# Sixteen filler matmuls as steps of TensorE's own order, and all step orders chosen anew, in a recurrent attention followed by a mixture of experts

## The chip, the cores and the metric

One core of one Trainium2 chip. The metric is the device time of one execution in microseconds; the median of several runs counts. PE is TensorE, ACT ScalarE, DVE VectorE, POOL GpSimd, SP SyncE. A "step" below is an entry of the kernel's plan: a handful of instructions that are issued together.

## The reference, cut to what matters

```
f = 1 / (1 + exp(-f_logit))                       # all of q, k, v, f: (4, 8, 768, 48)
for t in range(768):
    state = f[:, :, t, :, None] * state + einsum('bhd,bhe->bhde', k[:, :, t], v[:, :, t])
    y[:, :, t] = einsum('bhd,bhde->bhe', q[:, :, t], state)
x = y.transpose(0, 2, 1, 3).reshape(3072, 384)
p = domain_probs / (domain_probs.sum(-1, keepdims=True) + 1e-09)
for e in range(4):                                # w1[e]: 384 x 1024, w2[e]: 1024 x 384
    out += p[:, e:e+1] * (maximum(x @ w1[e], 0) @ w2[e])
```

## The kernel before, in words

The sequence is cut into six chunks (c = 0 to 5) of 128 tokens; a step's name ends in chunk and batch, so `q 0.2` is chunk 0, batch 2. Attention of a chunk is done in matrix form. For chunk 0 and each batch the steps are, in the order in which one needs the other:

- `ld f`, `ld k`, `ld q` (loads on SP's queue, 192 KB each) and `v issue` (POOL's queue, with a cast to bf16);
- `gate1`, `gate2` on ACT (exp and ln of the gate), then `cs` and `cq` on PE (cumulative sums over time, L388 to L399), then `exps` and `expq` on ACT;
- the products `k` and `q` (L434, L431), on DVE or POOL;
- `tpk`, `tpq` on PE (transposes, L443), `ev_tp` (their copy out of PSUM, on ACT or DVE), `at` on PE (scores, L474);
- `ev_at0`, `ev_at1`: scores out of PSUM with the causal mask, on DVE (L486); for the two named in `BYPOOL` ACT copies (L482) and POOL masks (`mask1`, L478);
- `y` on PE (L501), `ev_y`, `xt` on PE (transpose, L526), `ev_xt`: the chunk's part of x for the experts;
- `kv` on PE (L507), `ev_kv` on DVE (L514), four `sf` steps on POOL (L519, L522): the state for the next chunk.

The expert part has `h` (x times w1; in chunk 0's first expert twelve matmuls in a group, later three, L535; from chunk 1's second half `hs`, L567), `relu`, and either `o` (h times w2, L550) or seven products `p` (L626, L635) of a Strassen-like scheme with sums `s` of h and sums `t` of w2 on DVE. Attention of the next chunk runs among the experts of the last one. Weights come in twelve pieces `w 0` to `w 11` on POOL's queue: `w 0` and `w 1` serve `h 0.0`, `w 2` and `w 3` `h 0.1`, `w 4` and `w 5` the products `p 0.d0`, `w 6` `h 0.2`, `w 7` `p 0.d1`, `w 8` `h 0.3`. `pp` and `probs` prepare the expert probabilities, from `ld p`.

The order of the work is written out: `STEPS` holds for each of PE, ACT, DVE, POOL and DMA a list of step numbers. An engine runs its list strictly in that order, and which list a step is in says which engine does it. `Plan.run` walks the lists to give out buffers and the order of emission; `GATE` and `SEQ` name which of the loads a `v` issue waits for and in what sequence v and w are issued.

Fillers are matmuls of 128 x 128 by 512 on a constant tile (`busy`) into a PSUM bank that is kept free for them (`SPARE`) until the first `h`. They have no use but to keep PE at work. Before, they hang on other steps, as a count that is issued just ahead of the step:

```
FILL = ((("cs", "cq"), 6), (("tpq", "tpk"), 4))
for kinds, n in FILL:
    next(o for o in done if o.engine == "PE" and o.name.split()[0] in kinds).pad = n
for o in done:
    for _ in range(o.pad):
        nc.tensor.matmul(out=spare, lhsT=busy[:, 0:128], rhs=busy, start=True, stop=True)
    o.ins = o.emit(o.engine)
```

So six stand ahead of the first `cs` and four ahead of the first transposes (L1083).

Of the kernel before, what the change touches and what calls it, by code (L numbers as in the profile page):

```python
# [34 lines left out]
    ),  # L35
    "ACT": (
# [10 lines left out]
    ),  # L47
    "DVE": (
# [15 lines left out]
    ),  # L64
    "POOL": (
# [6 lines left out]
    ),  # L72
    "DMA": (
# [109 lines left out]
def kernel(  # L183
# [11 lines left out]
    nc = tc.nc  # L195
# [29 lines left out]
    P = Plan(rooms)  # L225
# [845 lines left out]
    for kinds, n in FILL:  # L1071
        next(o for o in done if o.engine == "PE" and o.name.split()[0] in kinds).pad = n
# [59 lines left out]
```

## Time and profile before

| | |
|---|---|
| median of three runs | 288.67 us (286.22, 288.67, 290.31) |
| profiled execution | 287.4 us; its span 285.7 us |
| mean granted PE clock | 0.994 |
| busy: PE, weight loads, DVE | 277.8 us (97%), 242.4 us (85%), 220.2 us (77%) |
| busy: ACT, POOL | 159.8 us (56%), 111.3 us (39%) |
| chain that ended last | PE 92%, SP's queue 3%, DMA 2% |
| HBM read, written | 31.51 MB, 4.72 MB |

The span runs from the first to the last instruction of the profiled execution; its own time is 1.7 us longer. Busy time of PE is counted from issue to a modelled end, so matmuls that follow each other overlap in it. "The head" below is what comes before the stretch in which PE has no idle time any more, that is, the first 24 us.

### The profile page before, as it was taken

What the parts mean: (1) busy time and instruction counts of PE and PEld (TensorE: products, weight loads), DVE (VectorE), ACT (ScalarE), POOL (GpSimd) and SP (SyncE); (2) the same over time, 40 slices, a digit from 0 to 9 for tenths busy, and PEclk for the clock granted to TensorE, in tenths of its full rate; (3) what the DMA queues carried; (4) which work ended last, traced back from release to release, by engine and by line L of the source; (5) the groups of instructions that cost most, each with busy time, mean ns of one, the idle gap of its engine ahead of it and who ended that gap; (6) DMA issues with size and microseconds to landing.
All of it is one profiled execution on the core that took longest, in us unless ns stands there. A gap on an engine that the chain in (4) does not pass through costs nothing.

```text
span 285.7 us, 7671 instructions
## 1 busy us (share of the span) xinstructions
PE 277.8 (97%) x3100; PEld 242.4 (85%) x3100; DVE 220.2 (77%) x463; ACT 159.8 (56%) x320; POOL 111.3 (39%) x189
## 2 busy tenths in 40 slices
PE   6989999999999999999999999999999999999994
PEld 3678676668987999999999999998998999999994
DVE  5769898987889799885888867866976888554873
ACT  5763366687874868463955838754723632534410
POOL 5759000658269540738607344375436000000000
PEclk9979999999999999999999999999999999999999
DMA  6999999999969989999799869997562080461003
GB/s 148 208 201 207 207 208 212 185 186 202 211 117 149 196 160 194 212 187 209 145 167 202 163 130 174 213 157 131 101 105 67 1 112 2 110 140 28 2 2 111
DMA packets 153847, 41.87 MB, mean 147 GB/s; under 512 B 144316, under 2 KB 153020, under 8 KB 153812
## 3 DMA queue, kind: packets, MB, share of 16 engines
q1 hardware_dynamic: 142548, 34.66, 62.8%
q0 software_dynamic: 11264, 6.72, 16.8%
q8 instruction: 24, 0.39, 0.6%
q14 instruction: 11, 0.09, 0.1%
HBM read 31.51 MB, written 4.72 MB: 127 GB/s over the span
## 4 chain that ended last, share of the span: by engine, by line
PE 92%; SPq 3%; DMA 2%; DVE 1%; issue 1%; ACT 0%; DVEq 0%
PE ps_m L567 33%; PE ps_m L626 29%; PE ps_m L535 11%; PE ps_m L550 6%; PE ps_m L635 5%; PE ps_m L474 2%; DMA q<-in_q_dram 2%; PE ps_m L501 2%; SPq L336 1%; PE ps_m L507 1%; PE ps_m L497 1%; SPq L338 1%; PE ps_m L384 1%; PE ps_m L443 1%; PE ps_m L526 0%
## 5 line engine op out<-in xcount | busy, mean ns | idle before, releaser
L567 PE MATMUL ps_m<-x,w_sb 128*128 128x256 bf16 x864 | 105.6, 273 | 0.0
L575 ACT ACTIVATE h<-ps_m 128x512 bf16<-128x512 f32 x98 | 54.8, 599 | 67.2 <-PE ps_m L567 47.1
L567 PEld LDWEIGHTS <-w_sb 128*128 128x128 bf16 x864 | 82.3, 98 | 9.0
L626 PEld LDWEIGHTS <-S 128*128 128x128 bf16 x584 | 48.5, 98 | 1.2
L654 DVE TENSOR_TENSOR o<-ps_m,o 128x192 f32<-128x192 f32 x92 | 30.7, 351 | 18.4 <-PE ps_m L626 17.0
L573 DVE TENSOR_SCALAR h<-ps_m 128x512 bf16<-128x512 f32 x46 | 31.0, 686 | 10.8 <-PE ps_m L567 10.6
L434 POOL TENSOR_TENSOR qk<-q,e 128x384 bf16<-128x384 f32 x19 | 22.7, 1197 | 38.7 <-ACT e L417 26.4
L626 PEld LDWEIGHTS <-h 128*128 128x128 bf16 x432 | 36.6, 98 | 0.9
L535 PE MATMUL ps_m<-x,w_sb 128*128 128x128 bf16 (+2 forms) x264 | 35.6, 283 | 0.0
L457 ACT ACTIVATE yb<-ps_m,pn 128x384 bf16<-128x384 f32 x49 | 26.3, 597 | 6.3 <-PE ps_m L501 6.1
L490 DVE TENSOR_TENSOR AT<-ps_m,mask 128x512 bf16<-128x512 f32 x40 | 25.7, 684 | 4.6 <-PE ps_m L474 4.5
L626 PE MATMUL ps_m<-ts_sb,S 128*128 128x192 bf16 x288 | 29.2, 246 | 0.0
L522 POOL TENSOR_TENSOR Sf<-Sf,egs 48x192 f32<-48x192 f32 x40 | 20.5, 517 | 21.9 <-DVE S L590 12.3
L626 PE MATMUL ps_m<-w_sb,h 128*128 128x192 bf16 x288 | 28.8, 246 | 0.0
L626 PE MATMUL ps_m<-w_sb,S 128*128 128x192 bf16 (+1 forms) x296 | 28.6, 244 | 0.0
L546 ACT ACTIVATE h<-ps_m 128x512 bf16<-128x512 f32 (+1 forms) x44 | 19.8, 489 | 15.3 <-PE ps_m L535 12.5
L535 PEld LDWEIGHTS <-w_sb 128*128 128x128 bf16 x264 | 21.6, 98 | 7.6
L590 DVE TENSOR_TENSOR S<-h 128x1024 bf16<-128x1024 bf16 x36 | 24.6, 694 | 2.5 <-ACT h L575 1.6
L417 ACT ACTIVATE e<-ps_m 128x384 f32<-128x384 f32 x40 | 23.4, 705 | 4.8 <-PE ps_m L384 4.8
L434 POOL TENSOR_TENSOR qk<-k,e 128x384 bf16<-128x384 f32 x19 | 18.9, 1000 | 10.3 <-DMA k<-in_k_dram 5.0
L550 PE MATMUL ps_m<-w_sb,h 128*128 128x384 bf16 x96 | 18.1, 326 | 0.0
L349 POOL DMA_DIRECT2D w_sb<-in_moe_w_dram x12 | 9.6, 801 | 21.2 <-DMA k<-in_k_dram 21.2
(95 smaller groups left out, 372.6 us busy)
## 6 DMA issues: line engine op xcount, KB each, us to landing
out_dram<-o SPq DMA_DIRECT2D x23, 192.0 KB, 2.4
q<-in_q_dram SPq DMA_DIRECT2D x10, 384.0 KB, 5.6
k<-in_k_dram SPq DMA_DIRECT2D x10, 384.0 KB, 5.2
v<-in_v_dram SPq DMA_DIRECT2D x10, 384.0 KB, 5.1
f<-in_f_logit_dram SPq DMA_DIRECT2D x9, 384.0 KB, 5.5
w_sb<-in_moe_w_dram POOLq DMA_DIRECT2D x8, 384.0 KB, 7.6
w_sb<-in_moe_w_dram POOLq DMA_DIRECT2D x4, 768.0 KB, 14.1
f<-in_f_logit_dram SPq DMA_DIRECT2D x6, 192.0 KB, 3.9
```

The source lines that it names most:

```text
L417: nc.scalar.activation(out=o, in_=i, func=AF.Exp, scale=1.0 if j else -1.0)
L434: return engines[eng].tensor_tensor(out=tl("qk", c, b)[:, j, :, 0:D].rearrange("t (i r) d -> t i r d", r=2), in0=tl("qk"[j], c, b // 2)[:, ...
L457: nc.scalar.activation(out=ys, in_=y, func=AF.Copy, scale=pe)
L490: nc.vector.tensor_tensor(out=tl("AT", c, b)[:, r].rearrange("s i t -> s (i t)"), in0=tl("A", c, b, r).rearrange("s i t -> s (i t)"), in1= ...
L535: nc.tensor.matmul(out=hp(c, e, fc, n0, n1, nf)[:, f], lhsT=w1_sb[:, e, kk, (fc + f) * 128:(fc + f + 1) * 128], rhs=tl("xT", c)[:, kk, n0: ...
L550: nc.tensor.matmul(out=tl("op", c, e, nt)[:, 0:Din], lhsT=tl("h", c, e, half_of(c, nt * T))[:, fc, nt * T:(nt + 1) * T], rhs=w2_sb[:, e, f ...
L567: nc.tensor.matmul(out=out_[:, f], lhsT=w1_sb[:, e, kk, (fc + f) * 128:(fc + f + 1) * 128], rhs=tl("xs", c, hf, p)[:, el, kk, :], start=(k ...
L573: nc.vector.tensor_relu(out=dst, in_=tl("hp", c, hf, p, el, fc))
L575: nc.scalar.activation(out=dst, in_=tl("hp", c, hf, p, el, fc), func=AF.Relu)
L590: return nc.vector.tensor_tensor(out=o, in0=in0, in1=in1, op=op)
L626: nc.tensor.matmul(out=out_, lhsT=lhs[:, f, :], rhs=rhs[:, f, cols], start=(first and el == 0 and f == 0), stop=(el == 1 and f == KH - 1), ...
L654: nc.vector.tensor_tensor(out=o, in0=src, in1=o, op=ALU.add)
```

## The change

The ten hanging fillers (`pad`, `FILL`) go. Sixteen become steps of their own, `fl 0` to `fl 15`, one matmul each, which stand in PE's list wherever the list puts them. All five lists are other ones (steps behind the fillers have numbers higher by 16). `BYPOOL` becomes "0.1 2.1": the second half of batch 0's scores, instead of batch 1's, is copied by ACT and masked by POOL. `SEQ` and `GATE`: `v 1` is issued ahead of `v 0`; `v 1` waits for `k 0.0` and `v 0` for `k 0.2` (before, `v 0` for `k 0.1` and `v 1` for `k 0.2`).

```diff
-        self.pad, self.number = 0, None
+        self.number = None
...
+    def filler():
+        return nc.tensor.matmul(out=spare, lhsT=busy[:, 0:128], rhs=busy, start=True, stop=True)
+
+    for i in range(FILLERS):
+        P.add(f"fl {i}", {"PE": 0.22}, lambda _: filler(), -190 + i, frees=[SPARE])
...
-    for kinds, n in FILL:
-        next(o for o in done if o.engine == "PE" and o.name.split()[0] in kinds).pad = n
...
-        for _ in range(o.pad):
-            nc.tensor.matmul(out=spare, lhsT=busy[:, 0:128], rhs=busy, start=True, stop=True)
...
-FILL = ((("cs", "cq"), 6), (("tpq", "tpk"), 4))
+FILLERS = 16
-SEQ = "v0 v1 v2 w0 v3 w1"
-BYPOOL = "1.1 2.1"
+SEQ = "v1 v0 v2 w0 v3 w1"
+BYPOOL = "0.1 2.1"
-GATE = {"v0": (0, "k", 1), "v1": (0, "k", 2)}
+GATE = {"v1": (0, "k", 0), "v0": (0, "k", 2)}
```

The lists of the head, with names in place of numbers. PE, before (`6 fl` and `4 fl` are the hanging ones) and after:

```
before: 6 fl, cs 0.1, cs 0.0, cq 0.1, cq 0.0, 4 fl, tpk 0.1, tpq 0.1, tpk 0.0, tpq 0.0, at 0.1, cs 0.3, at 0.0, cq 0.3,
        cs 0.2, cq 0.2, y 0.0, tpk 0.3, pp, tpq 0.3, tpk 0.2, y 0.1, tpq 0.2, xt 0.0, at 0.3, xt 0.1, kv 0.1, at 0.2,
        kv 0.0, h 0.0.0.128, y 0.3, h 0.0.0.0, kv 0.3, xt 0.3, y 0.2, xt 0.3, kv 0.2, h 0.0.4.0, xt 0.2, h 0.0.0.384 ...
after:  fl 11, 13, 1, 6, 4, 14, cs 0.0, cq 0.0, cs 0.1, cq 0.1, tpk 0.0, tpq 0.0, fl 10, fl 9, tpk 0.1, cs 0.3, tpq 0.1,
        cq 0.3, at 0.0, fl 5, at 0.1, fl 7, fl 3, fl 12, cs 0.2, cq 0.2, pp, tpk 0.3, y 0.1, kv 0.1, fl 8, tpq 0.3, fl 15,
        y 0.0, tpk 0.2, tpq 0.2, xt 0.1, at 0.3, xt 0.0, fl 2, at 0.2, fl 0, kv 0.0, h 0.0.0.0, y 0.3, h 0.0.0.128,
        kv 0.3, xt 0.3, y 0.2, xt 0.3, kv 0.2, h 0.0.4.128, xt 0.2, h 0.0.4.384 ...
```

SP's loads (all but `p` with chunk 0):

```
before: f1 f0 q1 k0 k1 k2 q0 f3 f2 k3 p q3 q2
after:  f0 f1 k0 f3 q0 k2 k1 q1 k3 f2 q3 p q2
```

POOL:

```
before: v issue 0, 1, 2, w issue 0, v issue 3, k 0.3, w issue 1, mask1 0.1, w issue 2, 3, 4, mask1 0.2, w issue 5, 6, 7,
        sf 0.0.0, sf 0.1.0, sf 0.3.0, sf 0.3.1, w issue 8 ...
after:  k 0.0, v issue 1, 0, 2, w issue 0, v issue 3, w issue 1, 2, mask1 0.0, w issue 3, 4, 5, mask1 0.2, sf 0.0.0,
        w issue 6, sf 0.3.0, sf 0.1.0, sf 0.0.1, sf 0.1.1, w issue 7, 8 ...
```

DVE and ACT:

```
before DVE: k 0.1, k 0.0, q 0.1, q 0.0, ev_tp 0.1, ev_tp 0.0, ev_at0 0.1, ev_at1 0.0, ev_at0 0.0, q 0.3, k 0.2, q 0.2,
            ev_tp 0.2, ev_at1 0.3, ev_at0 0.3, ev_at0 0.2, ev_y 0.3, ev_kv 0.0 ...
after DVE:  q 0.0, k 0.1, q 0.1, ev_tp 0.1, k 0.3, ev_at0 0.0, ev_at0 0.1, ev_at1 0.1, q 0.3, k 0.2, q 0.2, ev_tp 0.3,
            ev_tp 0.2, ev_at0 0.3, ev_at1 0.3, ev_at0 0.2, ev_y 0.3, ev_kv 0.0 ...
before ACT: gate1 0.1, gate2 0.1, gate1 0.0, gate2 0.0, exps 0.1, exps 0.0, expq 0.1, expq 0.0, gate1 0.3, gate2 0.3,
            gate1 0.2, gate2 0.2, exps 0.3, ev_at1 0.1, expq 0.3, exps 0.2, expq 0.2, ev_y 0.0, ev_tp 0.3 (twice) ...
after ACT:  gate1 0.0, gate2 0.0, gate1 0.1, gate2 0.1, exps 0.0, gate1 0.3, expq 0.0, exps 0.1, expq 0.1, gate2 0.3,
            ev_tp 0.0, exps 0.3, gate1 0.2, gate2 0.2, ev_at1 0.0, expq 0.3, exps 0.2, expq 0.2, ev_y 0.1, ev_tp 0.3 ...
```

Behind the head the lists hold the same steps in other orders, and some evictions have changed between ACT and DVE: PE's steps have moved by up to 28 places.

108 rows, old and new, of the table STEPS are left out of this document.

## The prediction

> **What bounds the kernel now.** I read the 40 slices of the page first, then the table by stage of the head, then the chain that ended last.
>
> ```profile
> PE   6989999999999999999999999999999999999994
> PEclk9979999999999999999999999999999999999999
> ```
>
> PE is full from the fourth slice (7.14 us each) to the last. Only the first three hold idle time or a low clock (the 7). Two-microsecond stages show the same:
>
> ```profile
> 12.00:14.00 2.00, 1.87 (x32) 1.52 (x29) 1.96 (x3) 1.97 (x7) 1.15 (x2) 1.00 2.05 196
> 14.00:16.00 2.00, 1.18 (x16) 0.98 (x16) 0.99 (x2) 1.76 (x6) 1.99 (x4) 1.00 1.41 208
> 16.00:18.00 2.00, 1.79 (x25) 1.43 (x27) 1.29 (x4) 1.06 (x2) 1.93 (x3) 0.72 1.68 189
> 18.00:20.00 2.00, 2.00 (x27) 1.46 (x27) 1.81 (x4) 0.96 (x3) 0.00 (x0) 0.50 1.33 200
> ...
> 28.00:30.00 2.00, 2.00 (x11) 0.94 (x10) 2.00 (x5) 0.24 (x1) 0.67 (x1) 1.00 1.14 213
> 30.00:34.00 4.00, 4.00 (x33) 2.70 (x32) 3.02 (x6) 2.31 (x5) 0.00 (x0) 1.00 1.24 203
> 34.00:40.00 6.00, 6.00 (x51) 4.23 (x49) 5.62 (x12) 4.36 (x10) 0.00 (x0) 1.00 1.19 208
> ```
>
> After the stage's length come busy times of PE, PEld, DVE, ACT, POOL, then the granted clock. Between 14 and 16 PE is busy for 1.18 us only; from 16.9 to 20.3 (the same table in quarters of a microsecond) the clock is 0.50. From 24 on PE has no idle time. So the end is set by when PE's dense stretch begins: whatever is saved ahead of it moves the end one for one, and an order behind it can only lose. What holds it back:
>
> ```profile
> 9.62 5.37 DMA q<-in_q_dram
> 15.14 0.86 issue
> 16.00 0.56 DVE qk L434
> 20.32 0.72 PE ps_m L535 x12
> ```
>
> The chain runs through SP's thirteen loads and a q that lands at 14.99 (9.62 + 5.37). The last q is issued at 10.3 and lands 6.1 later (longest landing of that line), at 16.4. Then DVE and PE have to carry the last two batches through products, transposes, scores, masks and the output, partly at half clock.
>
> **The change, part by part.**
>
> *Fillers.* The cold ones cost 0.46 us each:
>
> ```profile
> 1.52 2.74 PE L1083 MATMUL ps_m<-S 128*128 128x512 bf16 x6 [1.52 <-DVE S L231]
> 8.27 1.91 PE L1083 MATMUL ps_m<-S 128*128 128x512 bf16 x4
> ```
>
> No warm one is in the trace. Bounds: above 0.478 (1.91 / 4), below 0.215, from 512-column matmuls of line 535 at full clock (the chain has 1.29 us for six). I take 0.22. The first six stand ahead of everything and fill the wait for the first f, as before: nothing. Before, four stood together ahead of the transposes; now two (fl 10, 9) fill the wait for k 0.1 (the seventh load; the wait of DVE for the load in that place ended at 9.93): nothing. Four (fl 5, 7, 3, 12) fill the wait for cs 0.2, two (fl 8, 15) that for q 0.3 and k 0.2. These eight are covered by the loads; without that cover they would cost 8 x 0.22 = 1.8 us. The last two (fl 2, fl 0) lie in the busy part, among at 0.2 and kv 0.0: I charge 0.43.
>
> *Loads.* SP has the same thirteen, so I give each place in the queue the landing it had. k0 moves to the third place, f3 to the fourth, q0 to the fifth, q1 to the eighth, f2 to the tenth. The tenth was issued at 8.02 and landed 5.0 later: f2 at 13.1, not about 11.3. The thirteenth is still q2: 16.4. On POOL the v and w transfers keep their sequence but for v1 ahead of v0. Ahead of them now stands product k 0.0: exps 0.0 ends at 6.69, a product of that kind takes 1.00 on POOL, so the first v issue starts near 7.75 (before 7.91, waiting for k). No loss, as long as k0 lands before 6.7.
>
> *The later f2.* Two gates take 1.07 from start to end (ACT rows at 10.60 and 11.15): 14.15. Then cs 0.2 needs 0.58 on PE, while ACT does ev_at1 0.0 and expq 0.3. By the starts of the same steps in the rows (12.98, 13.56, 13.93, 14.36) they follow each other by 0.58, 0.37 and 0.43; exps 0.2 starts near 15.2 and expq 0.2 ends near 16.15. That is 0.25 ahead of q2's landing at 16.4. So the move is hidden; if f2 lands 0.5 late, it costs 0.25.
>
> *Mask and copies.* ev_at1 0.0 goes to ACT and its mask to POOL in place of 0.1's; w issues 3 to 5 stand behind that mask. It ends near 15.6 (ACT cast until 14.9, mask 0.66), and in the old order those issues began at 16.4 and the last went out at 21.4: no loss.
>
> *The clock.* PE's work from 10 to 19.5 in the new order, with the durations of the rows, leaves idle about 0.65 us ahead of cs 0.2 (13.5 to 14.2) and little else, where before 1.2 us was idle between 13.5 and 16.9, just ahead of the low clock. So I expect full clock from about 10 on. Bounds of what it is worth: at most half of the 3.4 us at 0.50, 1.7; at least nothing, if DVE and the loads set the pace. From tpq 0.2 (17.13) to the third group of 12 at line 535 (22.95) it was 5.82 us. Of this 3.17 were cold, so 1.59 goes; kv 0.1 has moved out ahead (0.2), two fillers are in (0.43): 4.45. q 0.2 again ends near 17.0, tpq 0.2 starts at 17.05, and the third group by PE alone at 21.5. DVE bounds it from the other side: ev_tp 0.2 at 17.5 instead of 17.77, then 0.69, then the three ev_at (2.10 together) until 20.3, not 20.73. Before, DVE then stood idle 0.85 for y 0.3, which was held by a matmul group on PE; now y 0.3 is due at 19.7 while DVE still works, and its copy (0.42) and the first ev_kv (0.73) follow until 21.45, kv 0.2 takes that bank, and the group starts at 21.7. I take 21.7: a gain of 1.25, between 0 and 1.7.
>
> A rule of the Trainium skill speaks against this part. TensorE: Matmul & The Clock Gate, Part 1, has the clock fall after an idle window of some 3.4 us and calls for no gaps longer than that. By it the old head, with 0.83 as its longest gap at that point, would never have cooled and fillers there would be worth nothing. The trace disagrees: 0.50 for 3.4 us.
>
> *The dense stretch.* The same 262.7 us of work (285.7 - 22.95) in another order. The loads don't come sooner, so starting 1.25 us earlier shrinks margins. Adding the steps' durations from 21.7 (0.65 for a group of three or twelve, 0.66 for a product), the first product p, which needs the sixth weight piece, comes at 29.7; that piece lands at 28.8 (issue 21.41 + 7.4). The tightest place is the second chunk's transposes: q 1.1 ran on POOL from 53.58 to 54.77, and tpq 1.1 stands at 53.9 in the new order. Its inputs come sooner too (cs 1.1 right after cs 1.0; one egs issue, 0.56, has left POOL's queue ahead of it), so I find 53.3 for its end, and 54.4 for k 1.1, wanted at 54.8. Such joints are worth 0 to 1 us lost; I take 0.3.
>
> Sum: span 285.7 - 1.25 + 0.3 = 284.75; the profiled execution took 287.4 for its 285.7, so 286.45. It was 1.3 below the median shown (288.67), within the runs' own 286.22 to 290.31. If those differ by how often PE ran cold, which no row shows, the new kernel has less to differ by; I stay with the profiled base: 286.4.
>
> **The rivals.**
>
> (a) *The clock still falls*, at another place of the head, or the gain is taken by DVE and the loads. For it: the stretch 14 to 16 waits for data whatever fills it, and the trace doesn't tell how full PE must be; 12 to 14 with 1.87 of 2 kept the clock, 14 to 16 with 1.18 lost it. The four fillers from fl 8 on would then cost 0.48 each, 1.9, of which half is hidden: 287.4 + 0.0 to 0.9, so 287.4 to 288.3. The same page says that the window runs freely, so the cold stretch can come elsewhere in another run; the one profile of before can't show that.
>
> (b) *The weights come late* and the kernel is slower. In the new order of POOL, w issue 6 stands behind mask1 0.2 and sf 0.0.0, and w issue 7 behind four state steps that wait for DVE. I put issue 7 near 26.3 instead of 22.2. If a piece of 768 KB needs its 14.1 us from issue, piece 7 lands at 40.4, its first product p 0.d1 is due at 38.8, and piece 8 (due at 41.4 for h 0.3.7) lands about 2 us late: PE stands 2 to 4 us, net of the gain 288.5 to 290.5. It decides from the point where an issue comes later than the end of the piece ahead of it. Against it: ten pieces were issued in bursts and kept the DMA share above 1 and some 200 GB/s in every stage to 40 us, so the 14.1 is mostly queueing; issue 7 at 26.3 is still ahead of piece 6's landing.
>
> (c) *The fillers save more*: PE is warm before 10 and the head's other waits close as well. PE would then start the third group near 20.7, when the second w piece (21.1) has not landed; so at most 1.85 before, 285.5.
>
> **How the numbers follow.** Forecast (0.3 to 1.7 faster than the profiled run) 0.58, (a) 0.2, (b) 0.17, (c) 0.05. The range, 284.0 to 290.0, takes in the gain's upper bound of 1.7 without joint losses (285.7) with as much again for runs below the profiled one (before had 1.2), and (b) up to 290; the forecast's own is 285.0 to 288.0. Two per cent, 5.8 us, is about what a measurement of this kernel can tell from no change. No case gains 5.8; (b) would lose it only if several pieces stall: faster 0.02, same 0.94, slower 0.04.
>
> **What would show it.** Right: a clock of 1.0 from about 10 us on without a gap, the third group of line 535 near 21.7, no PE idle time behind 24. Wrong in the clock: a 0.50 stretch between 10 and 24. Wrong in the loads: f2's gate behind 13.5, or the last q product behind 17. Wrong in the body: idle PE time with a weight DMA or POOL's qk as releaser, near 30, 39 or 54 us.

## The result: 3.4% slower

The changed kernel took 297.67 us (median of six runs, 294.37 to 301.07), the kernel before 287.39 (six runs, 285.29 to 290.31): a ratio of 1.0336, 95% interval 1.0251 to 1.042. Forecast were 286.4 and a range of 284.0 to 290.0; neither held. Ratios, here and below, leave out runs more than 1.5% above the fastest of the same kernel, so they aren't quite the ratios of the medians. The profiled execution took 298.07 us for a span of 296.3. Its page has the span, and PE with its clock in 40 slices (7.4 us each):

```profile
span 296.3 us, 7687 instructions
PE   6669999999899897999999999999999999999994
PEclk9978999999999999999999999999999999999999
```

The third group of 12 at line 535, first before, then after (timelines):

```profile
22.95 0.83 PE L535 MATMUL ps_m<-x,w_sb 128*128 128x128 bf16 x12
```

```profile
26.73 0.83 PE L535 MATMUL ps_m<-x,w_sb 128*128 128x128 bf16 x12
```

Two things are new. The clock still dips in the third and fourth slice, and PE, which was full from the fourth slice on, has an 8 in the eleventh, another in the fourteenth and a 7 in the sixteenth. The third group starts at 26.73, where it started at 22.95: in these two executions 3.8 us of the 10.6 us of span are lost ahead of it, in the head, and 6.8 behind it, in the body (296.3 - 26.73 = 269.6 against 262.75).

**The head of the changed kernel.** The table by stage (length; busy PE, PEld, DVE, ACT, POOL; granted clock; DMA share and GB/s):

```profile
16.00:18.00 2.00, 0.87 (x17) 0.59 (x16) 0.24 (x1) 0.48 (x1) 1.63 (x3) 0.98 1.61 188
18.00:20.00 2.00, 0.94 (x8) 0.66 (x8) 0.89 (x2) 0.32 (x1) 0.00 (x0) 0.50 1.36 202
20.00:22.00 2.00, 2.00 (x28) 1.64 (x26) 0.69 (x1) 1.15 (x3) 0.00 (x0) 0.50 1.24 204
24.00:26.00 2.00, 2.00 (x38) 2.00 (x36) 0.82 (x3) 1.04 (x3) 0.63 (x1) 0.81 1.31 203
```

From 16 to 20 PE is busy for 1.81 of 4 us, and the clock is 0.50 from 17.93 to 24.76 (the same table, finer), 6.83 us. What PE and DVE did meanwhile, by the timeline (start, duration, idle time before with its releaser), first DVE, then PE:

```profile
15.70 0.55 DVE L434 TENSOR_TENSOR qk<-k,e 128x384 bf16<-128x384 f32 x1
18.11 0.56 DVE L431 TENSOR_TENSOR qk<-q,e 128x384 bf16<-128x384 f32 x1 [1.87 <-DMA q<-in_q_dram]
18.59 0.42 DVE L325 COPY QK<-ps_m 112x512 bf16<-112x512 bf16 x1
```

```profile
16.49 0.38 PE L919 MATMUL ps_m<-S 128*128 128x512 bf16 x1
19.06 0.58 PE L443 MATMUL ps_m<-ident,qk 128*128 128x128 bf16 x4 [2.19 <-DVE QK L325]
```

The filler at 16.49 is followed by 2.19 us in which PE stands. The transposes behind it, tpq 0.3, had their input since the product q 0.3; but tpk 0.3 and tpq 0.3 share a PSUM tile, and PE waits until DVE has copied the tile's other half (ev_tp 0.3, line 325). In DVE's new list that copy stands behind q 0.2, and q 0.2 waits for the last q of the head, which landed at 18.02, and not at the forecast 16.4.

**The body of the changed kernel.** The waits of PE from 28 us on (total, times, longest):

```profile
PE ps_m L497 <- POOL sb L519: 2.6, 2, 2.1
PE ps_m L535 <- ACT e L417: 1.8, 1, 1.8
PE ps_m L497 <- ACT e L417: 0.7, 1, 0.7
PE ps_m L384 <- ACT e L417: 0.6, 1, 0.6
```

Together 5.7 us; in the same view of the kernel before nothing stands. Each goes back to the same step. On POOL, from 75 us (timeline):

```profile
75.91 1.00 POOL L434 TENSOR_TENSOR qk<-k,e 128x384 bf16<-128x384 f32 x1 [1.99 <-PE ps_m L635]
76.85 0.58 POOL L427 DMA_DIRECT2D egs<-e  x1
```

and on ACT:

```profile
77.85 0.38 ACT L546 ACTIVATE h<-ps_m 128x256 bf16<-128x256 f32 x1
80.84 1.16 ACT L417 ACTIVATE e<-ps_m 128x384 f32<-128x384 f32 x2 [2.62 <-DMA egs<-e]
```

The step egs (line 427) moves one row of an e buffer into egs by DMA, issued in POOL's queue. There are three e buffers. The next exps that writes that buffer (line 417, on ACT) must wait until the row is out: issued at 76.85, landed at 80.76, exps at 80.84. exps is also what empties its PSUM tile (line 384 had filled it at 78.32). The profile names exps as the releaser of PE's next h group (line 535), which starts at 82.06 as the second part of exps ends, after 1.77 us without work; the evictions of h (line 546), behind exps in ACT's list, wait with it. The other way through the same step is the state: Sf needs the row too. From the chain that ended last (start, duration, what):

```profile
110.47 2.96 DMA egs<-e
...
113.57 0.51 POOL Sf L522
...
114.13 0.57 POOL sb L519
...
114.74 0.20 PE ps_m L497
```

The issue at 76.85 is egs 1.1. In the kernel before it stood here on POOL:

```profile
55.71 0.61 POOL L427 DMA_DIRECT2D egs<-e  x1
```

It comes 21 us later now, behind products, copies of v and state steps. Likewise egs 1.0 went from 52.2 to 64.7, 1.3 from 63.0 to 87.6 and 2.0, the one in the chain above, from 79.8 to 110.5. Not all moved this way: 1.2 (82.1 to 69.6) and 2.1 (95.9 to 93.4) come sooner. The later start of the whole body, 3.8 us, is part of the delays.

### The profile page after: what moved, and what is told of

Read it like the earlier page. It is cut to its first block, busy times and chain, and to the rows that moved or that the text cites. A ratio compares the mean times of both kernels' runs of the same rounds, so it can differ in the third digit from the quotient of the medians.

```text
span 296.3 us, 7687 instructions
## 1 busy us (share of the span) xinstructions
PE 278.5 (94%) x3099; PEld 241.9 (82%) x3106; DVE 222.2 (75%) x466; ACT 159.6 (54%) x317; POOL 111.6 (38%) x189
## 4 chain that ended last, share of the span: by engine, by line
PE 56%; POOL 4%; DMA 2%; issue 1%; ACT 1%; DVE 0%; POOLq 0%; ACTq 0%
PE ps_m L567 27%; PE ps_m L626 25%; POOL qk L434 3%; DMA egs<-e 2%; POOL Sf L522 1%; PE ps_m L474 1%; PE ps_m L501 1%; PE ps_m L497 1%; PE ps_m L507 1%; PE ps_m L384 1%; POOL sb L519 1%; ACT e L417 1%; ACT yb L457 1%; DVE S L590 0%; POOL vb L325 0%
## 5 line engine op out<-in xcount | busy, mean ns | idle before, releaser
L575 ACT ACTIVATE h<-ps_m 128x512 bf16<-128x512 f32 x94 | 53.8, 599 | 61.9 <-PE ps_m L567 53.6
L654 DVE TENSOR_TENSOR o<-ps_m,o 128x192 f32<-128x192 f32 x92 | 31.0, 350 | 16.4 <-PE ps_m L626 15.2
L573 DVE TENSOR_SCALAR h<-ps_m 128x512 bf16<-128x512 f32 x50 | 33.6, 685 | 9.2 <-PE ps_m L567 9.0
L417 ACT ACTIVATE e<-ps_m 128x384 f32<-128x384 f32 x40 | 23.7, 707 | 18.2 <-DMA egs<-e 13.3
L434 POOL TENSOR_TENSOR qk<-k,e 128x384 bf16<-128x384 f32 x20 | 19.9, 999 | 32.5 <-DMA q<-in_q_dram 9.6
L546 ACT ACTIVATE h<-ps_m 128x512 bf16<-128x512 f32 (+1 forms) x49 | 22.7, 507 | 12.7 <-PE ps_m L535 12.6
L626 PE MATMUL ps_m<-w_sb,h 128*128 128x192 bf16 x288 | 29.5, 246 | 0.0
L626 PE MATMUL ps_m<-ts_sb,S 128*128 128x192 bf16 x288 | 28.5, 246 | 0.0
L590 DVE TENSOR_TENSOR S<-h 128x1024 bf16<-128x1024 bf16 x36 | 25.2, 707 | 4.0 <-ACT h L575 3.7
L459 DVE TENSOR_SCALAR yb<-ps_m,pn 128x384 bf16<-128x384 f32 x24 | 14.4, 612 | 6.4 <-PE ps_m L501 3.8
```

The lines of the kernel that those rows point to most:

```text
L417: nc.scalar.activation(out=o, in_=i, func=AF.Exp, scale=1.0 if j else -1.0)
L434: return engines[eng].tensor_tensor(out=tl("qk", c, b)[:, j, :, 0:D].rearrange("t (i r) d -> t i r d", r=2), in0=tl("qk"[j], c, b // 2)[:, ...
L573: nc.vector.tensor_relu(out=dst, in_=tl("hp", c, hf, p, el, fc))
L575: nc.scalar.activation(out=dst, in_=tl("hp", c, hf, p, el, fc), func=AF.Relu)
L590: return nc.vector.tensor_tensor(out=o, in0=in0, in1=in1, op=op)
L626: nc.tensor.matmul(out=out_, lhsT=lhs[:, f, :], rhs=rhs[:, f, cols], start=(first and el == 0 and f == 0), stop=(el == 1 and f == KH - 1), ...
```

## The experiments

Two theories stood at first. *Body:* the new order behind the head costs most of it, by the waits just shown. *Head:* the new head with its cold stretch costs most of it, and the body only follows it.

**Halves exchanged.** e1 takes the head of the kernel before with the new orders behind it, e2 the new head with the old orders behind it.

```
e1: PE, ACT, DVE, POOL, SP: steps of the head as before, the others in the order of after
e2: PE, ACT, DVE, POOL, SP: steps of the head as after, the others in the order of before
```

> The kernel before with its own head (loads, chunk 0's attention, the first expert's first layer in chunk 0, the issues of v and w, the ten hanging fillers), and all other steps on the engines and in the order of the kernel after. Theory 1 (the new body loses time by its own order, above all on POOL): about 6 us of PE idle time between 40 and 140 us stay, as in the profile after; 292 to 294. Rival (the body only pays for a late head: weights and chunk 1's loads come late): no idle time behind 24 us, 287 to 288.

> The kernel after with its own head (the sixteen fillers among it) and all other steps on the engines and in the order of the kernel before. Theory 1: only the head's loss stays; the third group of twelve at line 535 starts near 26.7 us instead of 22.95, PE has next to no idle time behind 30 us; 290 to 292. Rival: the late head brings the body's idle time with it whatever the order, 295 to 298.

e1: 297.3 us, ratio to before 1.0331 (1.0259 to 1.0404). e2: 288.46, 1.0042 (1.0009 to 1.0074). The body alone brings the whole loss; the head alone 0.4%. Both expectations missed the size, e1's by being too low and e2's by being too high: the body costs more and the head less than the 6.8 and 3.8 us of the changed kernel's profile. In e2's profile the clock stayed full from 10.49 us on, and the third group came at 23.20. PE's waits in e1 from 28 us on (its lines are one further down):

```profile
PE ps_m L536 <- ACT e L418: 2.0, 1, 2.0
PE ps_m L498 <- POOL sb L520: 1.8, 2, 1.3
PE ps_m L498 <- ACT e L418: 1.0, 1, 1.0
```

The same places, with the old head ahead of them. In e2 a single wait of 0.6 us, for PE itself, is left. What follows e1's longest wait is seen in its table by stage:

```profile
80.00:82.00 2.00, 1.27 (x12) 1.12 (x12) 0.01 (x1) 1.97 (x7) 1.18 (x2) 0.92 1.22 205
82.00:84.00 2.00, 2.00 (x23) 1.47 (x21) 1.84 (x4) 1.35 (x3) 1.64 (x3) 0.50 0.03 8
```

PE stood for 2.0 us until 80.73, and from 81.66 the clock was 0.50 for 3.4 us. So a wait can cost more than its length. It need not: the wait of 1.77 us in the same place of the changed kernel left the clock at 1.0.

**The copy ahead.** In the changed kernel, DVE's list alone:

```
-  ... q 0.3, k 0.2, q 0.2, ev_tp 0.3, ev_tp 0.2 ...
+  ... q 0.3, k 0.2, ev_tp 0.3, q 0.2, ev_tp 0.2 ...
```

> The kernel after with one edit on DVE: the copy ev_tp 0.3 stands ahead of product q 0.2 instead of behind it. Theory 2 (tpq 0.3 waits on PE for this copy, which waits in DVE's queue behind a product whose q lands at 18.0): PE's wait of 2.2 us at 16.9 goes, tpq 0.3 starts near 16.9, and the low clock that followed it is shorter or gone; third group near 24 instead of 26.7, 294 to 296 in all. Rival (the late landing of the last q alone sets the head's end): the wait only moves to tpq 0.2, third group at 26 to 26.7, 297 to 298.

294.37 us, 1.0256 (1.0199 to 1.0312). This interval overlaps the one without the edit (1.0251 to 1.042), so the times alone don't show a gain. PE's timeline at the same place:

```profile
16.13 0.38 PE L921 MATMUL ps_m<-S 128*128 128x512 bf16 x1
16.62 0.38 PE L445 MATMUL ps_m<-ident,qk 128*128 128x128 bf16 x4
```

tpq 0.3 follows its filler at once. In the profiled execution the clock stayed full through the head and the third group of 12 began at 21.95. But here the last q had landed sooner as well, at 16.91. The later runs with the new head tell the two apart. In e9 (below; it differs from the changed kernel in two buffer counts alone) the copy is in its place behind q 0.2, and the last q landed at 15.87. Its DVE, then its PE:

```profile
15.96 0.56 DVE L431 TENSOR_TENSOR qk<-q,e 128x384 bf16<-128x384 f32 x1 [0.39 <-DMA q<-in_q_dram]
```

```profile
16.91 0.38 PE L443 MATMUL ps_m<-ident,qk 128*128 128x128 bf16 x4 [0.82 <-DVE QK L325]
```

All seven profiles with the new head (times in us):

| run | copy ev_tp 0.3 | last q lands | third group | difference | clock at 0.50 |
|---|---|---|---|---|---|
| after | behind q 0.2 | 18.02 | 26.73 | 8.71 | 17.93 to 24.76 |
| e6 | behind | 17.86 | 26.54 | 8.68 | 17.70 to 24.53 |
| e2 | behind | 16.97 | 23.20 | 6.23 | not in the head |
| e9 | behind | 15.87 | 22.10 | 6.23 | not in the head |
| e3 | ahead | 16.91 | 21.95 | 5.04 | not in the head |
| e11 | ahead | 17.26 | 22.31 | 5.05 | not in the head |
| e10 | ahead | 18.24 | 23.29 | 5.05 | 11.24 to 14.66 |

In these seven the third group follows the landing of the last q at a fixed distance. With the copy ahead it is 5.05 us, with the copy behind 6.23, and 8.7 where the clock falls at that wait too. So the copy's place costs 1.2 us and the cold stretch 2.5, and a late q moves the start in either order. The copy's place lets PE wait for q; whether the clock then falls differs from execution to execution (2.19 and 2.26 us of waiting in after and e6, 1.24 and 0.82 in e2 and e9).

**The egs earlier.** In the changed kernel, POOL's list alone: every egs goes just ahead of the first product of its chunk and batch (for chunk 1, batch 0: ahead of q 1.1, the next product on POOL).

```
-  ... k c.b ... v copies, sf, sb ... egs c.b ...
+  ... egs c.b, k c.b ... v copies, sf, sb ...
```

> The kernel after with one edit on POOL: each issue egs (the transfer of the decay row out of an e buffer) stands just ahead of the first product of its chunk and batch, and no longer several steps behind it. Theory 1a (the late egs hold the three e buffers, so exps waits on ACT, evictions stand behind it, and PE behind those; the states wait for egs as well): PE's waits of 1.8, 0.7, 0.6 and 2.1 us at 82, 98, 104 and 115 us go but for 1 us in all; the head's loss stays; 291 to 293.5. Rival (the order of POOL's products and state steps, not of egs): at least 3 us of these waits stay, 294.5 to 298.

289.61 us, 1.0081 (1.0041 to 1.0122): of the 3.36% some 2.55 points, 7.3 us, go with this one kind of step. The profiled execution was the slowest of the six, 292.79 us, with a head as cold as in the changed kernel. All waits for e and sb are gone; what is left from 28 us on is

```profile
PE ps_m L569 <- DVE h L575: 0.8, 1, 0.8
PE ps_m L569 <- DMA x<-yb: 0.2, 1, 0.2
```

**Both together.** e11 is the changed kernel with the edits of e3 and e6, e10 is e2 with the edit of e3.

> The kernel after with both edits: ev_tp 0.3 ahead of q 0.2 on DVE, egs ahead of the products on POOL. If these two places hold the whole loss, PE has less than 1.5 us of idle time behind 24 us, and the time is 286 to 288.5. If there is a third cause in the new body, 289 to 293, and the idle time tells where.

> The new head with ev_tp 0.3 ahead of q 0.2 on DVE, and the old body. By the prediction's working of the head, third group near 21.9 us, no PE idle time behind it, 1 us faster than before: 285.5 to 286.5. Rival (as with the fillers alone, what the head wins in one profile is lost in the spread of the runs, or the loads move): within 0.5 us of before.

e11: 287.92, 1.0044 (1.0023 to 1.0064). e10: 287.75, 1.0028 (0.9997 to 1.006), not told apart from e2, and not the 1 us faster than before that was expected: in its profile the last q landed at 18.24, the clock was 0.50 from 11.24 to 14.66, and the third group came at 23.29 instead of 21.9. The page and PE's waits of e11:

```profile
PEclk9999999999999999999999999999999999999999
```

```profile
PE ps_m L569 <- DMA x<-yb: 0.6, 2, 0.4
PE ps_m L499 <- DVE h L575: 0.2, 1, 0.2
```

The two edits take back 2.9 points of 3.36. The egs edit is clear of the noise. The copy's isn't: it was worth 0.8 points in e3, 0.4 between e6 and e11 and 0.1 between e2 and e10, with overlapping intervals each time; its 1.2 us of the table are 0.4%. A rest of 0.4%, 1.3 us, stays, and 0.8 us of waits don't make all of it.

**Is it the buffer?** e9 gives the changed kernel a fourth e buffer; for its room two of the four QK buffers go.

```
-    "e": 3, "QK": 4
+    "e": 4, "QK": 2
```

> The kernel after, orders unchanged, with four e buffers in place of three (and two QK buffers in place of four, for the room). Theory 1a: ACT's waits for egs and with them PE's waits at 82 and 98 us go (2.5 us and whatever clock they cost), those for the state's cast at 104 and 115 stay; 294 to 296. Rival: the buffers are not it, PE's waits at 82 and 98 stay, 297 to 298.

297.52 us, 1.0374 (1.0322 to 1.0426): no better, where 294 to 296 were expected. PE's waits between 60 and 140 us:

```profile
PE ps_m L497 <- POOL sb L519: 1.8, 1, 1.8
PE ps_m L567 <- DMA x<-yb: 1.7, 3, 0.8
PE ps_m L626 <- DVE o L654: 0.3, 1, 0.3
```

The waits for ACT's e are gone, as the buffer theory has it, and the wait by way of the state stays, which needs the row whatever the number of buffers. But new waits for transposed x came in, here 1.7 us and later 2.54 and 0.93. With two QK buffers fewer the total says nothing on the worth of the e buffer.

**The converse.** e13 puts one egs late in the kernel before, which needs a product moved as well; e14 moves the product alone.

```
e13, POOL: -  egs 1.1 ... sf 1.1.0 ... q 2.0
           +  q 2.0, egs 1.1, sf 1.1.0
e14, POOL: -  sf 1.1.0 ... q 2.0
           +  q 2.0, sf 1.1.0
```

> The kernel before with two steps of POOL moved: product q 2.0 ahead of sf 1.1.0, and the issue egs 1.1 behind q 2.0 (it stood ahead of sf 0.1.1, some 17 us sooner). Theory 1a from the other side (a late egs holds the third e buffer and with it exps 2.1, ACT's queue and PE): egs 1.1 is issued near 73 us and lands near 76, exps 2.1 starts then and not at 75.1, PE waits 1 to 2 us near 77; 288 to 289.5. Rival (egs only hurts with the new body's other orders): within 0.4 us of the kernel of the next run.

> The kernel before with product q 2.0 ahead of sf 1.1.0 on POOL and egs 1.1 where it was: the measure for the run above. Both theories: no PE idle time near 77, within 0.5 us of before.

The wait came, where none was, if shorter than the 1 to 2 us expected. egs 1.1 was issued at 74.69 and landed at 78.09. ACT's timeline and PE's waits in e13:

```profile
78.11 1.17 ACT L419 ACTIVATE e<-ps_m 128x384 f32<-128x384 f32 x2 [1.50 <-DMA egs<-e]
```

```profile
PE ps_m L537 <- ACT e L419: 0.8, 1, 0.8
```

The time, 288.61 or 1.0023 (0.9976 to 1.0069), against 286.69 or 0.9989 (0.9951 to 1.0026) for the control, is too wide to resolve 0.8 us. What is shown is the way of the wait, not its price.

**The fillers.** e5 is the kernel before with the sixteen fillers as steps of PE's order and nothing else: six and four where they were, one ahead of at 0.1, one ahead of y 0.0, four ahead of tpq 0.3. e12 is the kernel before with none.

```
e12: -FILL = ((("cs", "cq"), 6), (("tpq", "tpk"), 4))
     +FILL = ()
```

> The kernel before, with its own orders, engines and load sequence, and sixteen fillers as steps of their own: six and four where they were, one ahead of at 0.1, one ahead of y 0.0 and four ahead of tpq 0.3, in the holes of PE at 11.1, 13.9 and 15.3 us. Theory 3 (PE's busy share sets the clock, and the clock was worth what the prediction said): no 0.50 stretch behind 10 us, third group near 21.6 instead of 22.95, 1 to 1.5 us faster than before. Rival (DVE and the loads set the head's pace): full clock, but the third group between 22.5 and 23.2, within 0.5 us of before.

> The kernel before without any filler, nothing else changed. Theory 3a (the ten fillers already keep the clock in most runs, six more had nothing left to win): full clock comes later or is lost in the head in nearly every run, mean granted clock 0.98 to 0.99, 288 to 290. Rival (the loads set the head's pace whatever the clock): within 0.5 us of before.

e5: 287.06 us, 0.9999 (0.9968 to 1.003). e12: 286.8, 1.0004 (0.9971 to 1.0038). Ten, sixteen or none make no difference clear of the noise, some 0.3%; both theories missed. The profiled execution of e12, in the stage in which the kernel before lost its clock:

```profile
14.00:16.00 2.00, 1.45 (x21) 1.16 (x19) 1.55 (x3) 1.53 (x6) 1.99 (x3) 1.00 1.63 192
16.00:18.00 2.00, 2.00 (x42) 1.66 (x42) 1.51 (x3) 1.83 (x4) 1.80 (x3) 1.00 1.74 188
```

Without a filler anywhere the clock stayed at 1.0 from 9.7 us on, where its record begins. And of 65 executions of the kernel before that ran beside these experiments, 29 had a mean granted clock of 0.997 or more and took 286.36 us in the median, 27 had 0.991 to 0.994 and took 287.32, and nine had 0.982 to 0.988 and took 289.14. One stretch of 3.4 us at 0.50 makes 0.994 of a span of 286. The profiled execution of before, 0.994 and 287.4 us, was of the second kind. If nothing else sets these groups apart, one such stretch, which the prediction meant to save, costs about 1 us, and 29 of the 65 executions have none.

## Why the prediction was wrong, by its own steps

**The dense stretch** is the step that failed: "Such joints are worth 0 to 1 us lost; I take 0.3." They cost 6.8 us in the profile, and 7.3 by the runs with and without the egs edit. The working looked at the right queue and read it with the wrong sign: "one egs issue, 0.56, has left POOL's queue ahead of it" was booked as time saved for q 1.1. Where the step went, and that it holds an e buffer until its row has landed, was not asked. The test at the end named "a weight DMA or POOL's qk as releaser, near 30, 39 or 54 us"; the releasers were ACT's e and POOL's sb, at 82, 98, 104, 115 and 138.

**The clock and the loads**, second: "Four (fl 5, 7, 3, 12) fill the wait for cs 0.2, two (fl 8, 15) that for q 0.3 and k 0.2", "The thirteenth is still q2: 16.4", and from them a gain of 1.25. The walk followed each input of tpq 0.3, but not the PSUM tile that it writes; the copy ev_tp 0.3 behind q 0.2 wasn't seen. And the last q came at 18.02. Of the 5.0 us by which the third group missed its 21.7, the table above gives 1.6 to the late q, 1.2 to the copy and 2.5 to the cold stretch, and 0.2 the other way. The rest of the walk held: with the copy ahead the third group came 5.05 us behind the last q, where the forecast has 5.3 (16.4 to 21.7). The prediction's own sign for this, "the last q product behind 17", showed: it began at 18.11. Rival (a) had the right symptom, a cold clock in another place of the head, and priced it at 0 to 0.9 us.

**The base**, third: the sum went from a profiled run with a cold stretch that 29 of 65 executions don't have. The prediction saw this ("which no row shows") and stayed with the profiled base. That its 287.4 is also the median of the six runs, 287.39, is luck. Even with the copy in its right place the new head gained nothing (e10).

**Rival (b)** gave the slower side, by late weights. Not so: piece 6 landed at 34.4 and piece 8 at 43.2, and PE waited for none of them. Its form was right, an issue held back in POOL's queue; it was egs, not a weight piece.

**What held.** The gates of f2 began at 12.96 (forecast 13.1), expq 0.2 ended at 15.8 (16.15), the first v issue started at 7.46 (7.75), the mask ended at 15.4 (15.6): the later f2, the product ahead of v and the moved mask were hidden. The old orders behind the new head (e2) cost 0.4%, so the old body bears a shifted start as assumed; it was the new body that didn't.

**Open.** The last q of the head landed between 15.4 and 18.2 us in these profiles, mostly later with the new loads (15.9 to 18.2) than with the old (15.4 to 17.5). Why wasn't tried. It matters: with the copy ahead the new head needs 5.05 us from that landing to the third group, the old one at full clock 5.4 to 6.4 (e5, e14, e12), and the later landing takes this back. Nor is the rest of 0.3 to 0.4% in e2 and e11 explained.

## What to carry to other kernels

When a queue is put in a new order, list for each moved step not only who consumes its result but which buffer it holds, and who queues behind the engine that waits for that buffer: here transfers of a single row each, issued up to 31 us later on POOL, reached PE by way of ACT and of the state, and cost 2.5%. The same holds for a PSUM tile of which two steps use one half each. And before a stretch of low clock is priced, look at the time and mean clock of several executions: a stretch that only some of them have is worth that much less on average.

## What the runs showed of the hardware

- **The clock went after some waits of 2 us and not after others.** It fell 0.93 us after the end of a wait of 2.0 us (e1), and in the changed kernel during one of 2.19. A wait of 2.13 us for sb, ended at 110.31, cost e3 its clock at 111.44; the same wait in the changed kernel, 2.07 us, ended at 114.74, did not. Nor does the busy share of a stage decide: the changed kernel kept the clock from 12 to 14 us with PE busy for 1.17 of 2, the kernel before lost it behind 1.18 of 2. The Trainium skill (TensorE: Matmul & The Clock Gate, Part 1) lets the clock fall after an idle window of some 3.4 us. By that rule none of these waits would have cost more than itself; the measurements disagree. The length of the cold stretches, 3.4 us (e1) and 6.83 (after), agrees with one and two such windows.
- **The clock changes on a grid.** In all 13 traces its changes lie whole multiples of 3.413 us apart, counted from a first one that comes anywhere from 4.17 (e14) to 10.88 us (e5, e6). So the same wait meets the grid in another place in each execution, which fits a stretch that comes and goes. Ahead of the first change the tables show 1.00 without a record: in the kernel before four matmuls of line 388 took 0.80 us at 5.08 and 0.50 at 11.76, both at a shown 1.00.
- **A small transfer isn't quick.** The seven egs rows that the changed kernel issued from 64.7 to 114.6 us took 2.7 to 3.9 us from issue to landing (median 3.35). A buffer that such a transfer reads is held for that long, behind whatever holds back its issue.
